# Sliding-window attention and gated MLP: w_in in two halves, three pairs turned by DMA, and another order for the first seventeen slots

## The chip, the cores and the metric

One core of one Trainium2 chip runs one launch. The time is the device time in microseconds; the figure of record is the median of several runs. TensorE (PE) does matmuls and transposes, ScalarE (ACT) the exponentials, the relu and some copies, VectorE (DVE) copies, normalisation and the gate's product, GpSimd (POOL) casts, masks and the weight loads, SyncE (SP) issues most DMAs.

## The reference

```python
scores = scale * np.matmul(q, k.transpose(0, 1, 3, 2))      # 8 batches, 8 heads, 576 x 64
rel = pos[:, None] - pos[None, :]
mask = (rel >= 0) & (rel < 128)
scores = np.where(mask, scores - slope[h] * np.abs(rel), -1e9)
attn = softmax(scores)
x = np.matmul(attn, v)            # to 4608 tokens x 512
h = x @ w_in                      # 512 -> 2048
g = h * np.clip(h + 3.0, 0.0, 6.0) / 6.0
out = g @ w_out                   # 2048 -> 512
```

## The kernel before

The attention goes by 32 slots g: a slot is a batch b = g // 4 and a pair of heads hp = g % 4. In a slot, queries and keys stand transposed in qTb and kTb (64 rows of each head, so a pair fills 128). A window of 128 means that a tile of 128 queries meets two key tiles: the diagonal one (scores into the PSUM tile scd, exponentials into pd) and the one before (sco, po). For batches 0 and 1 the slope and the mask of some tiles are added by matmuls with a table (tables_diag, tables_off); elsewhere POOL masks with affine_select. The products with v land in av, are divided by their sums (avs), turned so that the features lie on partitions, and stored in xT, a ring of four batches.

The MLP goes by nine token tiles nt of 512. Each has 16 up units (moe_up: 4 matmuls of 128x512 from xT and w_in_sb, then ACT's relu L470 and DVE's product L471 into gbuf) and 16 down units (moe_down: 4 matmuls from gbuf and w_out_sb; after each fourth a copy and a store). The list `units` fixes their order from ORDER, and `fill(n)` issues the next n, if the xT that they read is complete (`done`). Everything is issued in an order written out by hand: each engine runs its own instructions strictly in that order, and waits on semaphores.

Loads: the q and k of batch 0 come pair by pair (load_run, k on ACT's queue, q on SP's, eight loads in the order of the pairs 0 to 3), are cast to bf16 (prepare), turned by 36 PE transposes of 64x64 (transposes, L219) and copied to qTb and kTb (L220). Those of batches 1 and 2 come as four-head blocks (load_double, prepare_double, wide_double or double), those from batch 4 on by tokens and a transposing DMA (xbar). Each DMA waits for the eighth before it, whose semaphore it takes over, and SP issues strictly in order. The same space in ldbuf serves batch after batch, so a load also waits for the cast that reads the one before.

w_in comes in four quarters of 512 columns and w_out in four of 512 rows, cast by POOL's DMA queue (L166, L171). In batch 0, pd and po live in w_out_sb, in batch 1 in gbuf[1].

first_batch warms PE with 20 matmuls of 128x128 (L153), adds the tables of slot 0, warms with 10 more, then does transposes(0), scores, exponentials and so on by slot; all four exponentials must be in before attend(3) and back(3), which complete xT for the first up unit. back(g) turns avs by five PE transposes (L432) and one copy for slots 0 to 7, 10 and 11, and by a DMA transpose (L425) for the others; by_xbar tells which. second_batch does slots 4 to 8, segment the rest, one slot after the other, each with seven calls of fill.

Of the kernel before, what the change touches and what calls it, by code (L numbers as in the profile page):

```python
# [18 lines left out]
def kernel(  # L19
# [29 lines left out]
    NB_FULL = 2  # L49
    RING = 4 * S  # L50
# [5 lines left out]
    ident = perm.tile([128, 128], BF16)  # L56
    bias3 = perm.tile([128, 1], FP32)
# [22 lines left out]
    p4buf = [held.tile([128, 2, 128], BF16, name=f"p4buf{i}") for i in range(2)]  # L80
# [94 lines left out]
    def second_w_in():  # L175
        nc.gpsimd.memset(w_out_sb[:, 4, 0:1], 0.0)
        load_w_in(1)

# [24 lines left out]

    def prepare(g, copies):
        for nm, copy in zip("qk", copies):
            pr = prs.tile([128, RT * D], BF16, tag=f"pr{nm}", name="pr",
                          padded_shape=[128, 2 * RT * D])
            copy(out=pr, in_=runs[nm][:, g % NP, :])
            st[g, nm] = pr

    def transposes(g, copies):
        b, hp = divmod(g, NP)
        for nm, dst, copy in (("q", qTb[b % 2], copies[0]), ("k", kTb[b % 2], copies[1])):
            src = st.pop((g, nm))
            tp = ps_h.tile([128, RT, RP], BF16, tag="h", name="tp", padded_shape=[128, 16, 64])
            for t in range(RT):
                for e in range(2):
                    r = slice(e * D, (e + 1) * D)
                    nc.tensor.transpose(tp[r, t, :], src[r, ts(t, D)], ident[r, r])  # L219
            copy(out=dst[:, hp, :, :].rearrange("p j c -> p (j c)")[:, 0:S].rearrange(  # L220
                "p (a t) -> p a t", t=RT), in_=tp.rearrange("p t a -> p a t"))
# [52 lines left out]
    def rooms(g):  # L274
        b, hp = divmod(g, NP)
        if full(g):
# [81 lines left out]
    def exp_off(g, e):  # L358
        h = 2 * (g % NP) + e
        po, sc, p4 = st[g, "po"], st[g, "sco"], p4buf[g % 2]  # L360
# [13 lines left out]
    def av_matmuls(g, qts, where):  # L374
        b, hp = divmod(g, NP)
        vb = vbuf[b % 2]
        pd, po, p4 = st[g, "pd"], st[g, "po"], p4buf[g % 2]
# [135 lines left out]
    ORDER = [("UUDUDUUDUD", "UUDUDUDUD", "UDUDUDD", "UUDDDD"),  # L513
# [3 lines left out]
    for nt in range(1, n_nt + 1):  # L517
        ups, downs = iter(range(16)), iter(range(16))
        for c in "".join(ORDER[0 if nt == 1 else 2 if nt == n_nt else 1]):
            units.append((nt, moe_up, next(ups)) if c == "U" else (nt, moe_down, next(downs)))  # L520
# [36 lines left out]

    def first_batch():
        prepare(0, (V, A))
        warm_up(20)  # L560
        tables_diag(0)
        tables_off(0)
        warm_up(10)
        transposes(0, (V, A))
        scores_diag(0)
        prepare(1, (P, V))
        transposes(1, (V, V))
        scores_off(0)
# [12 lines left out]
        exp_full(2)
        scores_diag(3)
        scores_off(3)
        exp_full(3)
        cast_v(0, 0, V)
        cast_v(0, 1, P)
        load_w_in(0)
        cast_v(0, 2, V)
        cast_v(0, 3, V)
        cast_v(0, 4, P)  # L590
        for dp in range(2):
            for nm in "kq":
                load_double(1, dp, nm, nc.sync)
        load_tokens(1, "v")
        attend(0)
        attend(1)
        back(0)
        attend(2)
        back(1)
        prepare_double(1, 0, (P, P), early=second_w_in)  # L600
        attend(3)
        back(2)
        up_begin(0, 0, 3)
# [160 lines left out]
```

## Time and profile before

| what | value |
|---|---|
| three runs, median | 323.52 us (323.32 to 324.7) |
| profiled execution | 323.3 us |
| its span | 321.6 us |
| mean granted clock of PE | 0.998 |
| DMA issues from launch to landing, q and k of batch 0 | 3.7 to 7.3 us, median 5.4 |
| w_in quarters, issue to landing | 6.3 to 9.5 us, median 8.8 |
| xT by DMA transpose, first six | 2.4 to 4.3 us, median 3.0 |

The span runs from the first to the last instruction of the profiled execution; its time is 1.7 us longer. "Busy" on PE counts a matmul from its start to the modelled end of its result, so two matmuls in a row overlap in it, and a short wait between them can hide under the first one's end. What PE loses is therefore read from the starts. An idle time in square brackets names what ended it.

### The profile page before, as it was taken

How to read it: one execution, taken by the hardware profiler on the slowest of the kernel's cores; microseconds unless marked ns; L12 is line 12 of the kernel's file. 1: busy time of each engine (PE TensorE's matmuls, PEld its weight loads, DVE VectorE, ACT ScalarE, POOL GpSimd, SP SyncE). 2: the span in 40 equal slices, each digit the busy share in tenths (PEclk: the TensorE clock that was granted, in tenths of full speed). 3: DMA queues.
4: the chain of work that ended last, by engine and by line, in shares of the span. 5: the costliest groups of instructions: out<-in, count | busy, mean ns of one | idle time of the engine just before them, and what ended most of it. 6: DMA issues, size and time to landing. Idle time of an engine off the chain costs nothing.

```text
span 321.6 us, 7050 instructions
## 1 busy us (share of the span) xinstructions
PE 312.4 (97%) x2738; PEld 167.6 (52%) x2738; DVE 173.0 (54%) x338; ACT 195.6 (61%) x334; POOL 141.1 (44%) x249
## 2 busy tenths in 40 slices
PE   7889999999999999999999999999999999999996
PEld 5565465455555554554667654554554444444443
DVE  6667674554456555555555555555655455455510
ACT  3758976877767766766676667666764344244401
POOL 8455493594493767366745665463331000000000
PEclk9999999999999999999999999999999999999999
DMA  7999999899999999999999989922112200000112
GB/s 276 202 333 208 247 270 196 210 258 194 212 248 166 244 201 203 193 229 199 192 199 202 237 173 212 214 72 86 23 53 66 75 34 35 33 33 33 67 53 77
DMA packets 131425, 51.90 MB, mean 161 GB/s; under 512 B 118976, under 2 KB 123328, under 8 KB 131392
## 3 DMA queue, kind: packets, MB, share of 16 engines
q1 hardware_dynamic: 126160, 45.36, 66.2%
q0 software_dynamic: 4224, 4.19, 8.2%
q10 hardware_dynamic: 1008, 1.90, 1.6%
q8 instruction: 21, 0.34, 0.5%
q14 instruction: 12, 0.10, 0.1%
HBM read 36.70 MB, written 9.44 MB: 143 GB/s over the span
## 4 chain that ended last, share of the span: by engine, by line
PE 82%; DMA 10%; SPq 2%; POOL 2%; DVE 1%; ACT 1%; issue 1%; POOLq 0%
PE ops L501 37%; PE hps L451 33%; DMA w_out_sb<-in_moe_w_out_dram 5%; DMA ldbuf<-in_v_dram 3%; PE scd L296 3%; DMA ldbuf<-in_k_dram 2%; PE av L391 2%; SPq L112 2%; PE av L383 2%; PE sco L328 1%; PE ops L482 1%; PE w L153 1%; POOL w_out_sb L171 1%; PE tp L219 0%; ACT kTb L244 0%
## 5 line engine op out<-in xcount | busy, mean ns | idle before, releaser
L471 DVE SCALAR_TENSOR_TENSOR gbuf<-r,hps 128x512 bf16<-128x512 f32 x144 | 98.7, 687 | 102.5 <-ACT r L470 100.2
L470 ACT ACTIVATE r<-hps,bias 128x512 f32<-128x512 f32 x144 | 98.9, 689 | 88.9 <-PE hps L451 88.7
L451 PE MATMUL hps<-xT,w_in_sb 128*128 128x512 bf16 (+1 forms) x640 | 144.8, 358 | 0.5 <-ACT xT L438 0.3
L501 PE MATMUL ops<-w_out_sb,gbuf 128*128 128x512 bf16 x560 | 137.8, 379 | 0.3 <-DMA w_out_sb<-in_moe_w_out_dram 0.3
L451 PEld LDWEIGHTS <-w_in_sb 128*128 128x128 bf16 x640 | 59.2, 98 | 54.8 <-issue 0.8
L501 PEld LDWEIGHTS <-gbuf 128*128 128x128 bf16 x560 | 51.8, 98 | 56.7 <-issue 0.6
L354 POOL TENSOR_SCALAR_AFFINE_SELECT pd<-pd 128x512 bf16<-128x512 bf16 x48 | 29.7, 634 | 34.5 <-ACT pd L351 34.5
L364 POOL TENSOR_SCALAR_AFFINE_SELECT po<-po 128x512 bf16<-128x512 bf16 x48 | 30.3, 636 | 32.5 <-ACT po L361 32.3
L351 ACT ACTIVATE pd<-scd,bias_d 128x512 bf16<-128x512 f32 x48 | 31.7, 685 | 4.7 <-PE scd L296 4.7
L510 DVE COPY osb<-ops 128x512 f32<-128x512 f32 x33 | 22.7, 687 | 20.4 <-PE ops L501 20.2
L361 ACT ACTIVATE po<-sco,bias_o 128x512 bf16<-128x512 f32 x48 | 33.0, 688 | 0.0
L194 POOL CAST tbuf<-ldbuf 128x512 bf16<-128x512 f32 (+1 forms) x45 | 25.6, 614 | 16.7 <-DMA qTb<-tbuf 9.0
L402 DVE TENSOR_TENSOR avs<-av,rc 128x384 bf16<-128x384 f32 (+1 forms) x48 | 23.6, 491 | 1.6
L391 PEld LDWEIGHTS <-pd 128*128 128x128 bf16 x192 | 14.3, 97 | 8.3 <-issue 0.5
L383 PE MATMUL av<-vbuf,po 128*128 128x65 bf16 x192 | 18.0, 193 | 0.0
L391 PE MATMUL av<-vbuf,pd 128*128 128x65 bf16 x192 | 17.3, 194 | 0.3 <-ACT kTb L244 0.3
L187 POOL CAST vbuf<-ldbuf 128x1024 bf16<-128x1024 f32 x14 | 14.3, 1044 | 4.3 <-DMA ldbuf<-in_v_dram 4.3
L383 PEld LDWEIGHTS <-po 128*128 128x128 bf16 x192 | 14.3, 98 | 2.9 <-DVE avs L402 0.5
L367 ACT ACTIVATE p4buf<-sco,bias_d 128x64 bf16<-128x64 f32 x48 | 15.5, 324 | 0.0
L227 POOL CAST pr<-ldbuf 128x576 bf16<-128x576 f32 x20 | 12.9, 670 | 5.0 <-DMA ldbuf<-in_k_dram 3.1
L296 PE MATMUL scd<-qTb,kTb 64*128 64x128 bf16 x256 | 12.7, 219 | 1.7 <-DVE kTb L220 0.9
L296 PEld LDWEIGHTS <-kTb 64*128 64x128 bf16 x256 | 7.2, 94 | 13.4 <-issue 9.7
(96 smaller groups left out, 217.4 us busy)
## 6 DMA issues: line engine op xcount, KB each, us to landing
out_dram<-osb SPq DMA_DIRECT2D x33, 256.0 KB, 2.4
ldbuf<-in_v_dram SPq DMA_DIRECT2D x32, 256.0 KB, 5.6
ldbuf<-in_q_dram SPq DMA_DIRECT2D x20, 256.0 KB, 4.9
ldbuf<-in_k_dram SPq DMA_DIRECT2D x16, 256.0 KB, 4.5
ldbuf<-in_q_dram SPq DMA_DIRECT2D x12, 288.0 KB, 7.3
ldbuf<-in_k_dram SPq DMA_DIRECT2D x12, 288.0 KB, 7.6
w_in_sb<-in_moe_w_in_dram POOLq DMA_DIRECT2D x4, 512.0 KB, 8.8
w_out_sb<-in_moe_w_out_dram POOLq DMA_DIRECT2D x4, 512.0 KB, 11.6
```

Of the source, the lines that this page charges most:

```text
L194: nc.gpsimd.tensor_copy(out=tbuf[:m, :, j, :], in_=s[:m, j, :, :].rearrange("p (i e) d -> p i (e d)", e=2))
L296: nc.tensor.matmul(scd[:, e, ts(j, 128)], lhsT=kT[r, j, :], rhs=qT[r, j, :], start=first, stop=first or j == 3)
L351: nc.scalar.activation(out=pd[:, e, :, :].rearrange("p j c -> p (j c)"), in_=sc[:, e, :], func=ACT.Exp, bias=bias_d[:, h:h + 1], scale=scale)
L354: nc.gpsimd.affine_select(out=pd[:, e, :, :], in_=pd[:, e, :, :], pattern=[[0, 4], [1, 128]], channel_multiplier=-1, base=0, compare_op=AL ...
L361: nc.scalar.activation(out=po[:, e, :, :].rearrange("p j c -> p (j c)"), in_=sc[:, e, :], func=ACT.Exp, bias=bias_o[:, h:h + 1], scale=scale)
L364: nc.gpsimd.affine_select(out=po[:, e, :, :], in_=po[:, e, :, :], pattern=[[0, 4], [-1, 128]], channel_multiplier=1, base=-1, compare_op=A ...
L383: nc.tensor.matmul(out_av, lhsT=po[:, e, qt % 4, :], rhs=vb[:, qt - 1, h, :], start=True, stop=False)
L391: nc.tensor.matmul(out_av, lhsT=d, rhs=vb[:, qt, h, :], start=(qt == 0), stop=True)
L451: nc.tensor.matmul(hps[:, lo:hi], lhsT=w_in_sb[:, ks, ts(ms, 128)], rhs=xT[:, ks, ds(src, hi - lo)], start=(ks == 0), stop=(ks == n_ks - 1))
L470: nc.scalar.activation(out=r6, in_=hps, func=ACT.Relu, bias=bias3[:, 0:1], scale=1.0 / 6.0)
L471: nc.vector.scalar_tensor_tensor(out=gts[nt][:, ms, :], in0=r6, scalar=1.0, in1=hps, op0=ALU.min, op1=ALU.mult)
L501: nc.tensor.matmul(ops[nt, sub], lhsT=gts[nt][:, ms, ts(sub, 128)], rhs=w_out_sb[:, ms, :], start=(ms == 0), stop=(ms == n_ms - 1))
```

## The change

first_batch, second_batch and the part of segment up to slot 19 are replaced by a list of steps, PLAN, one step a line. run_plan calls a small function for each. A step's own line names its operands (slot, token tile and unit, PSUM bank, engine: V is DVE, P is POOL, A is ACT). Copies and the PE work that they follow are separate steps now. From slot 20 on the loop of segment goes on as before.

- w_in is loaded by `wp 0 0 4` and `wp 1 0 4`, 128 rows by four k-blocks by 1024 columns each.
- `bx 5`, `bx 6` and `bx 4` give slots 4 to 6 back by a DMA transpose on SP; slot 7 (`bk 7`) stays on PE. 15 transposes of 128x128 and three copies L438 go.
- PE's order begins with 20 warm-up matmuls, the diagonal tables of slot 0 and the transposes of k of pair 2 (`t0 2 k`); then tables of slot 1, q of pair 1, seven warm-ups, k and q of pair 0.
- POOL begins with one memset and the cast `c0 2 k P`. The other memsets come later.
- The eight loads of q and k of batch 0 stay in their order. The v of batch 0 is no longer loaded right behind them, but between the loads of batch 1.
- Batch 0 is normalised into a room in gbuf[0] (avs0), by slot for query tiles 0 to 2 and by rows for the others; the last 64 tokens of it are turned for all slots at once (`br`, `er`).
- Up and down units have another order in token tiles 0 to 2; p4buf has four buffers.
- The steps in short: c0, t0, e0 are cast, PE transposes and copy of one operand of a batch-0 pair; pd, dt, de the same for a four-head block; td, to the tables, sd, so the scores, xt, xd, xo the exponentials, md a mask; vf, vr, vl, at the products with v, nf, nr, nl, na their normalisation; bf, ef and bk, ek turning and copying to xT; u, ur, um the matmuls, relu and product of an up unit (ub its first matmuls only), d a down unit; wu warm-up, mem and cv, vt, ct memsets and casts; ldd, ldt loads on SP; wp, wout the weight loads on POOL.
- Steps that aren't called (`sel`, `lw`, `vu` and others) are left out below.

```diff
+    NB_ROOM = 2
...
-    p4buf = [held.tile([128, 2, 128], BF16, name=f"p4buf{i}") for i in range(2)]
+    p4buf = [held.tile([128, 2, 128], BF16, name=f"p4buf{i}") for i in range(4)]
...
-    def second_w_in():
-        nc.gpsimd.memset(w_out_sb[:, 4, 0:1], 0.0)
-        load_w_in(1)
...
+    avs0 = gbuf[0].rearrange("p m c -> p (m c)")[:, ds(11 * NT, NP * NQ * 128)].rearrange(
+        "p (g j e d) -> p g j e d", g=NP, j=NQ, e=2)
...
-        if full(g):
+        if g < NB_ROOM * NP:
...
-    ORDER = [("UUDUDUUDUD", "UUDUDUDUD", "UDUDUDD", "UUDDDD"),
+    ORDER = [("UUDUDUUDUDUUDUDUDUDUDUDUDDUUDDDD",),
...
-        for c in "".join(ORDER[0 if nt == 1 else 2 if nt == n_nt else 1]):
+        for c in "".join((ORDER[0 if nt == 1 else 2 if nt == n_nt else 1]) if nt != 2 else "DDDDUUDUDUDUDUUDUDUDUDUUDUDUDDUU"):
...
-    def first_batch():
-        prepare(0, (V, A))
-        warm_up(20)
-        tables_diag(0)
-        tables_off(0)
-        warm_up(10)
-        transposes(0, (V, A))
...
-        attend(3)
-        back(2)
-        up_begin(0, 0, 3)
-        back(3)
-        wide_double(1, 0, "q", V)
...
+    def s_c0(g, nm, eng):
+        pr = prs.tile([128, RT * D], BF16, tag=f"pr{nm}", name="pr",
+                      padded_shape=[128, 2 * RT * D])
+        C[eng](out=pr, in_=runs[nm][:, g % NP, :])
+        st[g, nm] = pr
...
+    def s_t0(g, nm, tag):
+        src = st.pop((g, nm))
+        tp = psum(tag, RT * RP, BF16).rearrange("p (t a) -> p t a", t=RT)
+        for t in range(RT):
+            for e in range(2):
+                r = slice(e * D, (e + 1) * D)
+                nc.tensor.transpose(tp[r, t, :], src[r, ts(t, D)], ident[r, r])
+        st["t", g, nm] = tp
...
+    def s_e0(g, nm, eng):
+        dst = (qTb if nm == "q" else kTb)[0]
+        C[eng](out=dst[:, g, :, :].rearrange("p j c -> p (j c)")[:, 0:S].rearrange(
+            "p (a t) -> p a t", t=RT), in_=st.pop(("t", g, nm)).rearrange("p t a -> p a t"))
...
+    def s_ldd(b, dp, nm, e):
+        nc.sync.dma_start(out=ldbuf["qk".index(nm)][:, ds((2 * dp + e) * RT * D, RT * D)],
+                          in_=src_of[nm][b, ds(4 * dp, 4), :, :].rearrange(
+                              "(i e) (a t) d -> e a i (t d)", e=2, t=RT)[e])
...
+    def normed(av, to, n):
+        rc = small.tile([128, 4, 2, 1], FP32, tag="rcn", name="rcn")
+        nc.vector.reciprocal(rc[:, 0:n], av[:, :, :, D:W])
+        nc.vector.tensor_tensor(out=to, in0=av[:, :, :, 0:D],
+                                in1=rc[:, 0:n].to_broadcast([128, n, 2, D]), op=ALU.mult)
...
+    def s_vf(g, tag):
+        av = st["vf", g] = quads(tag, 3)
+        av_matmuls(g, range(3), lambda qt, e: av[:, qt, e, :])
...
+    def s_vl(g):
+        av = st["vl"] = quads("sc", 4)
+        av_matmuls(g, range(4), lambda qt, e: av[:, qt, e, :])
...
+    def s_bf(g, tag):
+        tp = st["bf", g] = psum(tag, 512, BF16)
+        for j in range(4):
+            nc.tensor.transpose(tp[:, ts(j, 128)],
+                                avs0[:, g, j, :, :].rearrange("p e d -> p (e d)"), ident)
...
+    def s_ef(g, lo, n, eng):
+        C[eng](out=xT[:, g, ds(lo, n)], in_=st["bf", g][:, ds(lo, n)])
...
+    def s_u(nt, ms, tag):
+        hps, n = st.get(("u", nt, ms), (None, 0))
+        if hps is None:
+            hps = psum(tag, 512)
+        up_mms(nt, ms, n, n_ks, hps)
+        st["u", nt, ms] = hps, n_ks
+        at[0] += 1
...
+    def s_ur(nt, ms):
+        r6 = st["r", nt, ms] = rpool.tile([128, NT], FP32, tag="r6", name="r6")
+        nc.scalar.activation(out=r6, in_=st["u", nt, ms][0], func=ACT.Relu, bias=bias3[:, 0:1],
+                             scale=1.0 / 6.0)
...
+    def s_um(nt, ms):
+        gts[nt] = gbuf[nt % 2]
+        nc.vector.scalar_tensor_tensor(out=gts[nt][:, ms, :], in0=st["r", nt, ms], scalar=1.0,
+                                       in1=st["u", nt, ms][0], op0=ALU.min, op1=ALU.mult)
...
+    def s_wp(i, k0, n):
+        nc.gpsimd.dma_start(out=w_in_sb[:, ds(k0, n), ts(i, 1024)],
+                            in_=moe_w_in[ds(k0 * 128, n * 128), ts(i, 1024)].rearrange(
+                                "(k p) f -> p k f", p=128))
...
+    def s_bx(g):
+        b, hp = divmod(g, NP)
+        nc.sync.dma_start_transpose(
+            out=xT[:, hp, ds(b % 4 * S, SP)].rearrange("p (j c) -> p j c", j=NQ),
+            in_=st[g, "avs"].rearrange("p j e d -> p (j e d)"))
...
+    def run_plan(text):
+        for line in text.split("\n"):
+            if line.strip():
+                name, *args = line.split()
+                STEPS[name](*(int(a) if a.isdigit() else a for a in args))
...
+    PLAN = """
+mem 1
+c0 2 k P
+c0 1 q V
+wu 20
+td 0
+c0 0 k A
+ldd 1 0 q 1
+t0 2 k av
+ldt 0 v 1
+td 1
+ldd 1 0 k 0
+e0 2 k V
+c0 1 k P
+t0 1 q o
+mem 2
+e0 1 q A
+wu 7
+t0 0 k h
+ldt 0 v 3
+e0 0 k A
+c0 0 q V
+t0 0 q h
+t0 1 k h
+e0 0 q A
+ldd 1 0 q 0
+e0 1 k V
+c0 3 q P
+c0 3 k P
+t0 3 q o
+sd 0
+xt 0
+t0 3 k h
+sd 1
+xt 1
+c0 2 q P
+t0 2 q h
+pd 1 0 q 0 V
+wp 0 0 4
+to 0
+e0 2 q V
+so 0
+mem 3
+pd 1 0 q 1 P
+ldt 0 v 0
+td 2
+e0 3 k V
+ldt 0 v 2
+sd 2
+xo 0
+ldd 1 1 k 0
+to 1
+cv 0 0 V
+xt 2
+cv 0 2 P
+so 1
+xo 1
+to 2
+so 2
+mem 5
+dt 1 0 q 0 9 sc
+cv 0 1 V
+ldd 1 0 k 1
+xo 2
+vf 0 av
+nf 0
+vf 2 h
+ldd 1 1 q 0
+pd 1 0 k 0 V
+e0 3 q A
+ldd 1 1 k 1
+ldd 1 1 q 1
+td 3
+sd 3
+vf 1 av
+nf 1
+cv 0 3 A
+vr 0 3 3 h
+ldt 0 v 4
+nf 2
+de 1 0 q 0 9 A
+xt 3
+nr 0 3 3
+to 3
+so 3
+bf 1 o
+ef 1 0 512 V
+pd 1 0 k 1 P
+dt 1 0 k 0 9 sc
+xo 3
+mem 0
+vl 3
+nl 3
+ldd 2 0 k 1
+bf 2 h
+bf 0 o
+ef 0 0 512 V
+bf 3 av
+de 1 0 k 0 9 A
+wp 1 0 4
+sd 5
+sd 4
+mem 4
+ef 3 0 256 A
+ef 3 256 256 A
+pd 1 1 k 0 P
+ef 2 0 512 V
+xd 5 0
+u 0 0 h
+u 0 1 o
...
+u 0 9 h
...
+at 5
+u 0 10 o
+ldt 2 v 0
+na 5
+bx 5
+xd 7 0
+xd 7 1
+um 0 8
+ur 0 10
+at 6
+na 6
+ldd 3 0 k 0
+ldd 2 1 k 0
+u 0 5 h
+mem 7
+md 7 0
+md 7 1
+pd 2 0 k 1 P
+bx 6
+pd 2 0 q 0 V
+dt 2 0 k 0 5 av
+de 2 0 k 0 5 A
+to 7
+so 7
+xo 7
+um 0 10
+md 4 1
+at 4
+ur 0 5
+vt 2 0
+na 4
+u 0 15 o
+ur 0 15
+dt 2 0 k 5 9 av
+um 0 5
+u 0 14 h
+ldd 2 1 q 0
+pd 2 0 q 1 P
+dt 2 0 q 0 9 sc
+at 7
+de 2 0 k 5 9 V
+de 2 0 q 0 9 A
+u 0 12 h
+um 0 15
+na 7
+ur 0 14
+um 0 14
+wout 0
+pd 3 0 k 0 P
+bx 4
+sd 8
+xd 8 1
+ub 1 0 3 av
+bk 7 sc
+xd 8 0
+ek 7 V
+sd 9
+pd 2 1 k 0 P
+ur 0 12
+u 1 5 h
+pd 2 1 q 0 P
+pd 2 1 q 1 V
+dt 2 1 q 5 9 sc
+ct 3 q 0
+xd 9 1
+ldd 2 1 k 1
+xd 9 0
+md 8 1
+u 1 3 o
+ur 1 5
+um 0 12
+u 1 0 av
...
+u 1 4 av
+de 2 1 q 5 9 A
+pd 2 1 k 1 P
+dt 2 1 k 0 5 h
+d 0 0 0 h
+wout 3
...
+um 3 12
+"""
...
-        load_tokens(0, "v")
...
-        memsets_later()
-        first_batch()
-        second_batch()
-        fill(2)
-        segment(2 * NP, G, lambda g: FILLS.get(g, (1, 1, 1, 2, 0, 1, 2)))
+        run_plan(PLAN)
+        done[0] = 20 - 1
+        segment(20, G, lambda g: FILLS.get(g, (1, 1, 1, 2, 0, 1, 2)))
         done[0] = G
```

1002 lines of the change are left out of this document (881 added, 121 removed).

## The prediction, made before the run

> **What bounds the kernel now.** I read the page first: busy times, then the slices, then the start by timeline.
>
> ```profile
> PE 312.4 (97%) x2738; PEld 167.6 (52%) x2738; DVE 173.0 (54%) x338; ACT 195.6 (61%) x334; POOL 141.1 (44%) x249
> ...
> PE   7889999999999999999999999999999999999996
> ```
>
> PE is busy for 312.4 of 321.6 us, and only the first three slices and the last are below nine tenths. So the change can win little beyond what PE loses early. The windows say how much is visibly idle:
>
> ```profile
> 0.00:20.00 20.00, 16.08 (x322) 11.57 (x323) 12.75 (x45) 11.01 (x13) 11.94 (x29) 1.00 0.98 250
> 20.00:45.00 25.00, 24.21 (x280) 14.01 (x277) 16.72 (x26) 21.00 (x33) 16.05 (x24) 1.00 1.12 273
> 45.00:60.00 15.00, 14.19 (x138) 8.08 (x135) 8.97 (x16) 11.62 (x21) 7.26 (x13) 1.00 1.09 181
> ```
>
> Columns after the length: PE, weight loads, DVE, ACT, POOL, granted clock, DMA share, GB/s. PE idles 3.9 us in the first 20 us, 0.8 and 0.8 in the next stretches. ACT is busy 21.0 of 25 us from 20 to 45: there a second engine is near its limit. From 120 to 300 us PE has no idle time at all, so a delay made before that is carried to the end.
>
> The start, PE's timeline first, then POOL's and ACT's:
>
> ```profile
> 1.43 2.31 PE L153 MATMUL w<-ident 128*128 128x128 bf16 x20 [1.43 <-POOL ident masks.py:199]
> 3.54 1.06 PE L271 MATMUL scd<-tab,ident 128*128 128x512 bf16 x2
> ...
> 5.24 1.27 PE L153 MATMUL w<-ident 128*128 128x128 bf16 x10
> 6.45 0.76 PE L219 MATMUL tp<-ident,pr 64*64 64x64 bf16 x36
> 7.94 0.40 PE L296 MATMUL scd<-qTb,kTb 64*128 64x128 bf16 x8 [0.74 <-ACT kTb L220]
> ```
>
> ```profile
> 7.66 1.63 POOL L208 CAST pr<-ldbuf 128x576 bf16<-128x576 f32 x2 [0.46 <-DMA ldbuf<-in_q_dram]
> ```
>
> ```profile
> 4.72 0.67 ACT L208 CAST pr<-ldbuf 128x576 bf16<-128x576 f32 x1 [0.18 <-DMA ldbuf<-in_k_dram]
> 7.24 0.64 ACT L220 COPY kTb<-tp 128x576 bf16<-128x576 bf16 x1 [1.85 <-PE tp L219]
> 8.38 1.02 ACT L348 ACTIVATE w_out_sb<-scd 128x1024 bf16<-128x1024 f32 x1 [0.49 <-PE scd L296]
> ```
>
> The reader is to see that pair 0 of k is there at 4.72 (its cast waits for the load), that PE begins transposes at 6.45, and that the first exponential runs at 8.38. POOL's row is the cast of q of pair 2, then of k of pair 2: it ends at 7.66 + 1.63 = 9.29, so k of pair 2 is castable at about 8.6. By the landings in the trace, k of the pairs 0 to 3 arrives at 4.70, 6.23, 8.47 and 9.46. The first run of dense up units starts at 23.88 us, 15.5 us behind the first exponential.
>
> **The change, part 1: the start.** PE works in order, and behind the 20 warm-ups and two table matmuls now stands `t0 2 k`, whose input is POOL's `c0 2 k`. The load order is unchanged, so that cast runs from 8.5 to 9.2 (0.67) and the first transposes come at 9.2, not 6.45; PE stands still from about 4.5. What follows, at the rows' durations: 18 transposes 0.4, copy `e0 2 k` on DVE 0.76 (to 10.4); meanwhile PE does tables and `t0 1 q`; `wu 7` needs the bank that e0 2 k frees, 0.4, `t0 0 k` 0.4 (to 11.4); ACT copies k and q of pair 0 one behind the other, 2 x 0.64 (to 12.8, `c0 0 q` on DVE waits behind e0 2 k and is done at 11.0, in time); `sd 0` 0.4. First exponential at 13.3, 4.9 late.
>
> That is at the full rate. The rows of the start show PE at half rate: a 128x128 matmul each 107 ns from 1.43 to 6.2, and 56 ns for the same shape later. It took 4.8 us of work without a break until the faster rate showed. The change works 3.0 us without a break and then waits 4.7. At half rate the five PE pieces between 9.2 and `sd 0` (0.4, 0.43 tables, 0.4, 0.4, 0.4 and the warm-ups) double, which moves the first exponential to about 15.2. Bounds 13.3 and 15.2; I take 14.5, nearer the slow end, since nothing shows the fast rate after so short a run.
>
> The Trainium skill, "TensorE: Matmul & The Clock Gate", Part 1, says that the array is at half rate until about 3.4 us of sustained work and falls back after an idle window as long. By it the end near 15.2 holds and the sum below grows by 0.7; the trace agrees with its two rates (107 and 56 ns), and no run so far shows the falling back.
>
> **Part 2: from the first exponential to the first up unit.** ACT's order is fixed: six exponentials of 1.02, `e0 3 q` 0.64, `cv 0 3` 0.67, `de 1 0 q` 1.11, two exponentials more: 10.6 us with little waiting, since tables and scores of a slot (0.9) fit under another's exponential. Then `vl 3` 0.7, normalising 0.2 + 0.8, `bf` 0.45, two ACT copies of 0.37: 2.9. First dense up unit at 14.5 + 13.5 = 28.0. Before it was 15.5 us behind the first exponential, so 2 us of waits are won back here. 28.0 - 23.9 = 4.1 late. But PE then has less left: 15 transposes L432 of 56 ns (0.84) never come; the rest (two four-head transposes and two sets of scores done early, the last query row and three begun up matmuls still owed) about cancels to 0.3 against. So the true lag is 4.1 - 0.5 = 3.6 us (2.4 at the full rate, 4.3 at half).
>
> **Part 3: w_in in halves.** Twice the bytes, the same 512 pieces. A quarter took 6.3 to 9.5 us to land; two issued together, at 27.83 and 28.56, were both in at 37.98, 10.2 us from the first. A half is bounded by one quarter's best, 6.3, and two times the worst, 19.0; I take 10.2, the row with the same bytes. `wp 0` stands behind `c0 2 q` on POOL, so at 14, landing at 24 (20 to 33), needed at 28. `wp 1` stands behind `pd 1 0 k 1` and is issued at about 24.5, landing at 34.7 (31 to 43.5), needed by `u 0 9`, seven units, two four-head transposes and a set of scores behind the first: 28 + 8 = 36. Cost nothing, cover 1.3 us; the late ends would cost 5 to 7.
>
> **Part 4: slots 4 to 6 by DMA.** Three ACT copies of 0.64 go, in the stretch where ACT is at 21.0 of 25 us. Added are three issues of 1.2 on SP. SP waits with `bx 5` for na 5, with `bx 6` for na 6, with `bx 4` for na 4; behind them stand the loads of batches 2 and 3, whose consumers come 5 us later or more. What is late next is `ub 1 0 3`, whose first matmul reads slot 4. From at 4 to there PE has `u 0 15`, `u 0 14`, `u 0 12` (0.86 each), at 7 0.53, 14 transposes 0.8, `sd 8` 0.3: 4.2 us. Normalising takes 1.0 and the landing 2.4 to 4.3 (as much as 7.3, as loads in a full queue take): 3.4 to 8.3. I take 4.0, the median row of 3.0, as SP stood waiting before it and its queue has emptied: nothing.
>
> **Part 5: the middle.** Adding up the starts in PE's timeline from 24 to 92 us, in ten places a matmul starts 0.18 to 0.49 us later than the one before it needs, 3.1 us in all; three of them, 0.98, are the backs and four-head transposes between 43.9 and 48.3, and one of 0.49 waits for w_out at 58.5, here:
>
> ```profile
> 59.05 1.02 PE L501 MATMUL ops<-w_out_sb,gbuf 128*128 128x512 bf16 x4 [0.33 <-DMA w_out_sb<-in_moe_w_out_dram]
> ```
>
> The first down unit now stands behind 23 up units, not 18, so that wait has cover; the new backs take the 0.98. Against it, `ur 0 0` is behind four exponentials of 0.69 on ACT. Bounds: 3.1 won, or the three loads and casts of part 4 that come late lose the 2.8 of those exponentials. I take 1.3 won.
>
> **Sum.** 323.3 (profiled execution) + 3.6 - 1.3 + 0 + 0 = 325.6. The median is 0.2 above the profiled execution: 325.8.
>
> **The rivals.** Nothing: the full rate holds (lag 2.4) and the middle gives 2.3 back: 323.5. For it: from 120 us on PE is closed, and the ten places are there to be closed. Against it: it needs the good end twice.
>
> Faster, by one mechanism: the third load on ACT's queue lands with the first. Place: `c0 2 k`. If k of pair 2 came at 4.7, the casts would be done at 5.4, the chain 3.8 us sooner and at the rate that unbroken work gives: first exponential 9.5, first up unit 23.0, lag -1.4; with 1.3 from the middle 323.5 - 2.7 = 320.8. It decides if the landing is before about 6.5. For it: all eight loads are launched within 1.4 us of each other. Against it: 4.70, 6.23, 8.47, 9.46, in order.
>
> Slower by more: a transfer comes behind its cover, `wp 1` for `u 0 9` or `bx 4` for `ub 1 0 3`. Price 1 to 7; by the middle of either 3.5: 329.3. For it: the DMA share is 1.0 to 1.1 there, and half a matrix waits for its last piece. Against it: both have 0.2 to 1.3 us of cover by the median rows.
>
> **How the numbers follow.** Forecast 0.46 (its own range 323.8 to 327.6), nothing 0.25, slower by more 0.16, faster 0.13. A measurement of this kernel can tell about 0.5%, 1.6 us, from no change: 321.9 to 325.1. Of the forecast 0.38 lies above that, 0.07 within; nothing gives 0.23 within, 0.01 on either side. Slower 0.38 + 0.16 + 0.01 = 0.55, within 0.30, faster 0.15. The range for 8 in 10 takes in the bounds of the start and part of either outer case: 321.0 to 329.6.
>
> **What would show it.** PE's first transposes at 9.2 with an idle time before them that ends with POOL's cast; matmuls at 107 ns still behind them; the first exponential at 13.3 to 15.2; the first dense up unit near 28; no idle time of PE that ends with w_in or xT's transposing DMA; fewer gaps between 43 and 60 us. I am wrong if the first transposes come before 7 us, if the first up unit comes before 25, or if over 3 us come back in the middle.

## The result, and the profile after

The changed kernel takes 335.78 us (median of four runs, 333.72 to 337.7), the kernel before beside it on the same chip 323.82 us: a ratio of 1.0365, with a 95% interval of 1.0299 to 1.0431. It is 12 us slower, above the range that was forecast. The profiled execution took 335.69 us, its span is 334.0.

The page of the changed kernel first: the span, the busy times, and in 40 slices PE's busy share and granted clock.

```profile
span 334.0 us, 6941 instructions
...
PE 311.3 (93%) x2680; PEld 169.0 (51%) x2720; DVE 171.3 (51%) x345; ACT 197.4 (59%) x337; POOL 135.3 (41%) x242
...
PE   3988994799999999899999999999999999999996
...
PEclk9997999699999999999999999999999999999999
```

PE is busy about as long as before (311.3 us against 312.4; some forty matmul records are missing in this trace), but the span is 12.4 us longer, so PE lost time standing still. The loss has two places: the first slice, and the slices from 50 to 67 us. In two slices the clock is below 9 tenths, each time just behind a wait. PE's timeline names the waits (start, length, and in brackets the idle time and what ended it):

```profile
8.69 0.69 PE L620 MATMUL bank<-ident,pr 64*64 64x64 bf16 x18 [4.09 <-POOL pr L611]
...
25.93 0.68 PE L756 MATMUL wide<-ident,pr 128*128 128x128 bf16 x9 [1.05 <-POOL pr L747]
...
60.14 1.44 PE L433 MATMUL bank<-xT,w_in_sb 128*128 128x512 bf16 x3 [6.13 <-DMA xT<-avs]
...
62.58 0.61 PE L433 MATMUL bank<-xT,w_in_sb 128*128 128x512 bf16 x1
...
137.57 1.24 PE L433 MATMUL bank<-xT,w_in_sb 128*128 128x512 bf16 x4 [1.10 <-DMA xT<-avs]
```

The first row is the start: `t0 2 k` waits for POOL's cast of the third load of k. The third is the large one: the first matmul of token tile 1 (`ub 1 0 3`) waits 6.13 us for slot 4, which `bx 4` brings by the transposing DMA. The first exponential, from ACT's timeline, and the cast of batch 1 behind the wait at 25.93, from POOL's:

```profile
14.40 1.94 ACT L330 ACTIVATE w_out_sb<-scd 128x1024 bf16<-128x1024 f32 x2 [0.73 <-PE scd L278]
```

```profile
25.21 0.66 POOL L747 CAST pr<-ldbuf 128x576 bf16<-128x576 f32 x1 [6.52 <-DMA ldbuf<-in_k_dram]
```

POOL stood still for 6.5 us until that load of k was in. It had been issued at 15.49, and the chain of waits has its whole way, as it has that of `bx 4`:

```profile
15.49 9.60 DMA ldbuf<-in_k_dram
...
51.44 8.66 DMA xT<-avs
```

The windows of the changed kernel (length, then busy time of PE, weight loads, DVE, ACT and POOL, granted clock, DMA share, GB/s):

```profile
20.00:30.00 10.00, 7.80 (x128) 5.46 (x127) 5.47 (x14) 7.17 (x11) 4.68 (x9) 0.85 0.94 253
53.50:65.00 11.50, 5.15 (x34) 2.73 (x35) 3.13 (x5) 4.11 (x7) 6.20 (x10) 0.70 1.21 208
```

In the kernel before, PE was busy for 9.35 us of the first of these windows and 11.04 us of the second, at a clock of 1.00 in both.

To see where the 12 us arise I use a lag: the time at which PE starts an instruction, less the time at which the kernel before started the one with equally much PE work left. (Up to 50 us it reads about 0.8 too low for kernels that give slots 4 to 6 back by DMA: the fifteen transposes are no work of theirs.)

| kernel (profiled execution) | 30 us | 50 us | 66 us | 105 us | 150 us |
|---|---|---|---|---|---|
| changed | 5.5 | 5.3 | 12.9 | 10.7 | 12.6 |
| changed, slots 4 to 6 back on PE (e1) | 4.0 | 5.2 | 4.3 | 2.8 | 3.3 |
| the order alone (e9) | 4.1 | 5.1 | 4.5 | 4.1 | 4.7 |
| start's queues mended (e15) | 2.0 | 4.9 | 4.0 | 2.5 | 3.2 |

So the changed kernel loses 5.3 at the start, 7.6 from 50 to 66 us, wins 2.2 back until 105, loses 1.9 more until 141 (1.10 of it in the last row of the timeline above), and nothing from there on: 323.3 + 12.6 = 335.9, against 335.7 profiled.

### The profile page after: what moved, and what is told of

The parts are those of the page before. It is cut to its first block, busy times and chain, and to the rows that moved or that the text cites. A ratio compares the mean times of both kernels' runs of the same rounds, so it can differ in the third digit from the quotient of the medians.

```text
span 334.0 us, 6941 instructions
## 1 busy us (share of the span) xinstructions
PE 311.3 (93%) x2680; PEld 169.0 (51%) x2720; DVE 171.3 (51%) x345; ACT 197.4 (59%) x337; POOL 135.3 (41%) x242
## 4 chain that ended last, share of the span: by engine, by line
PE 83%; DMA 9%; issue 1%; POOL 1%; DVE 1%; ACT 1%; SPq 0%; POOLq 0%
PE ops L483 24%; PE hps L433 21%; PE bank L433 14%; PE bank L791 9%; DMA xT<-avs 4%; DMA ldbuf<-in_k_dram 3%; PE scd L278 2%; PE av L373 2%; PE av L365 2%; PE sco L310 2%; DMA kTb<-tbuf 1%; PE ops L464 1%; DMA out_dram<-osb 1%; PE wide L756 1%; PE bank L620 1%
## 5 line engine op out<-in xcount | busy, mean ns | idle before, releaser
L452 ACT ACTIVATE r<-hps,bias 128x512 f32<-128x512 f32 x83 | 57.2, 689 | 65.6 <-PE hps L433 64.6
L483 PE MATMUL ops<-w_out_sb,gbuf 128*128 128x512 bf16 x354 | 87.5, 379 | 1.5 <-issue 1.0
L453 DVE SCALAR_TENSOR_TENSOR gbuf<-r,hps 128x512 bf16<-128x512 f32 x83 | 57.1, 688 | 59.9 <-ACT r L452 59.0
L433 PE MATMUL hps<-xT,w_in_sb 128*128 128x512 bf16 (+1 forms) x390 | 82.5, 344 | 0.2
L433 PE MATMUL bank<-xT,w_in_sb 128*128 128x512 bf16 x228 | 60.2, 387 | 8.3 <-DMA xT<-avs 7.2
L784 DVE SCALAR_TENSOR_TENSOR gbuf<-r,bank 128x512 bf16<-128x512 f32 x61 | 41.0, 684 | 31.6 <-ACT r L779 31.3
L779 ACT ACTIVATE r<-bank,bias 128x512 f32<-128x512 f32 x61 | 41.2, 690 | 19.9 <-PE bank L433 18.4
L791 PE MATMUL bank<-w_out_sb,gbuf 128*128 128x512 bf16 x177 | 43.3, 379 | 0.1
L346 POOL TENSOR_SCALAR_AFFINE_SELECT po<-po 128x512 bf16<-128x512 bf16 x24 | 15.2, 636 | 20.2 <-ACT po L343 20.2
L904 POOL TENSOR_SCALAR_AFFINE_SELECT po<-po 128x512 bf16<-128x512 bf16 x24 | 15.2, 636 | 19.7 <-ACT po L898 17.4
L937 POOL CAST tbuf<-ldbuf 128x512 bf16<-128x512 f32 (+1 forms) x25 | 14.6, 613 | 12.5 <-issue 7.4
L898 ACT ACTIVATE po<-sco,bias_o 128x512 bf16<-128x512 f32 x24 | 16.4, 688 | 3.0 <-PE sco L310 3.0
```

The source lines that it names most:

```text
L433: nc.tensor.matmul(hps[:, lo:hi], lhsT=w_in_sb[:, ks, ts(ms, 128)], rhs=xT[:, ks, ds(src, hi - lo)], start=(ks == 0), stop=(ks == n_ks - 1))
L452: nc.scalar.activation(out=r6, in_=hps, func=ACT.Relu, bias=bias3[:, 0:1], scale=1.0 / 6.0)
L453: nc.vector.scalar_tensor_tensor(out=gts[nt][:, ms, :], in0=r6, scalar=1.0, in1=hps, op0=ALU.min, op1=ALU.mult)
L483: nc.tensor.matmul(ops[nt, sub], lhsT=gts[nt][:, ms, ts(sub, 128)], rhs=w_out_sb[:, ms, :], start=(ms == 0), stop=(ms == n_ms - 1))
L779: nc.scalar.activation(out=r6, in_=st["u", nt, ms][0], func=ACT.Relu, bias=bias3[:, 0:1], scale=1.0 / 6.0)
L784: nc.vector.scalar_tensor_tensor(out=gts[nt][:, ms, :], in0=st["r", nt, ms], scalar=1.0, in1=st["u", nt, ms][0], op0=ALU.min, op1=ALU.mult)
```

## The experiments

Each kernel ran beside the kernel before. Ratios are to that kernel, with their 95% interval. Edits are to the changed kernel where nothing else is said.

### The three slots that go back by DMA

**e1_backs_pe**: slots 4 to 6 back on PE, the rest as changed.

```diff
-bx 5
...
+bk 5 av
+ek 5 A
...
-bx 6
+bk 6 av
+ek 6 A
...
-bx 4
+bk 4 av
+ek 4 A
```

> Slots 4 to 6 go back by five PE transposes and an ACT copy each, as before the change; all else as changed (335.8 us). Theory A, the first matmul of token tile 1 waits for slot 4's transposing DMA (6.1 us idle, then half rate): the wait and some 2 us at half rate go, 15 transposes of 56 ns (0.84) come back: 328.5. Rival B, the queue of SP is late as a whole, and q of batch 2's second block (landed 59.4) is waited for instead, a few steps on: only about 3 us are won, 332.5.

Measured: 327.98 us, 1.0135 (1.0097 to 1.0174). The transposing DMA costs 7.8 of the 12 us by the medians, 7.4 by the ratios. PE is busy for 10.92 of the 11.5 us from 53.5 to 65, at a clock of 1.00.

**e2_wout_late**: the first quarter of w_out is issued after `bx 4`, not ahead of it.

```diff
-wout 0
 pd 3 0 k 0 P
 bx 4
...
 pd 2 1 q 0 P
+wout 0
 pd 2 1 q 1 V
```

> The first w_out load is issued later on POOL, behind a cast that needs the landing of batch 2's q block, so that nothing of w_out moves while slots 5, 6 and 4 are transposed by DMA. Theory C, the weight load takes the DMA engines from SP's queue: slot 4 lands within 4.3 us of its issue instead of 8.7, PE waits 1 us or less, 329.5, unless the down units then wait for w_out. Rival, the transposing DMA itself is slow or serial: slot 4 lands as late as now, 335.8 or more.

Measured: 331.94 us, 1.0266 (1.0228 to 1.0303). PE's timeline of this kernel, the lines with waits:

```profile
55.04 0.81 PE L433 MATMUL bank<-xT,w_in_sb 128*128 128x512 bf16 x3 [1.64 <-DMA xT<-avs]
63.69 1.04 PE L791 MATMUL bank<-w_out_sb,gbuf 128*128 128x512 bf16 x4 [0.79 <-DMA w_out_sb<-in_moe_w_out_dram]
68.29 1.89 PE L791 MATMUL bank<-w_out_sb,gbuf 128*128 128x512 bf16 x8 [2.04 <-DMA w_out_sb<-in_moe_w_out_dram]
75.85 2.75 PE L791 MATMUL bank<-w_out_sb,gbuf 128*128 128x512 bf16 x12 [1.13 <-DMA w_out_sb<-in_moe_w_out_dram]
```

The wait for slot 4 falls from 6.13 to 1.64 us, but the down units now wait three times for w_out, 4.0 us in all. The view of the DMA issues says the same in one row each (what, queue, kind, how many, size, median us from issue to landing), for 45 to 62 us. The changed kernel:

```profile
q1 hardware_dynamic: 6111, 2.58, 79.4%
q0 software_dynamic: 528, 0.52, 28.5%
...
xT<-avs SPq DMA_TRANSPOSE x3, 7.1
```

and this one:

```profile
xT<-avs SPq DMA_TRANSPOSE x3, 4.2
```

The same three transposes land in 4.2 us, by the median, without a w_out quarter under way and in 7.1 us with it. `bx 5` took 2.7 us in both kernels, ahead of that load; `bx 6` and `bx 4` took 4.9 and 4.2 us here, 7.15 and 8.66 in the changed kernel. The two queue rows of the changed kernel give packets, MB and the packets' share of 16 engines' time. The weight load's 528 packets of about 1 KB take 28.5% of 17 us on 16 engines, so 147 ns each; SP's 6111 of about 0.4 KB take 79.4%, so 35 ns each. Together that is 107.9%, more than the engines have: packets overlap in time, and these are durations, not times in which an engine served one packet alone.

**e5_keep_warm**: 100 warm-up matmuls where PE waits for slot 4.

```diff
+wu 100
 ub 1 0 3 av
```

> The changed kernel, with 100 warm-up matmuls of 128x128 on PE ahead of the first matmul of token tile 1, where PE waits 6.1 us for slot 4. Theory F, the 2 us lost behind that wait are PE at half rate after it stood still: the wait stays, the matmuls behind it come each 216 ns at once, 333.8. Rival, the 2 us are other waits of the same queue: 335.8.

Measured: 331.01 us, 1.0248 (1.0203 to 1.0292), 4.8 us less than the changed kernel by the medians and 3.8 by the ratios, by work that serves nothing. PE's timeline of this kernel at the place:

```profile
51.52 5.76 PE L156 MATMUL w<-ident 128*128 128x128 bf16 x100
57.34 0.81 PE L433 MATMUL bank<-xT,w_in_sb 128*128 128x512 bf16 x3
```

The three matmuls behind the wait take 0.81 us here and 1.44 in the changed kernel. From 57 to 65 us this kernel's lag doesn't grow, where the changed kernel's grows by 2.0 between 60.1 and 66.6: so 2.0 of the 4.8 us is PE's lower clock behind the wait. Another 2.1 was there ahead of the edit (lag at 50 us without the added matmuls 3.2, not 5.3): this kernel had no wait at 25.93 and a clock of 1.00 from 20 to 30. The load of k behind that wait was issued at 14.70 and landed at 23.39 us here, 15.49 and 25.09 in the changed kernel. Why, with the same instructions up to there, stays open; the changed kernel's four runs themselves spread over 4 us.

**e6_before_xbar**: the kernel before, with slots 4 to 6 back by DMA and the loads of batches 2 and 3 moved behind the three transposes.

```diff
-        return g >= XB and g != XB + 2 and g != XB + 3
+        return NP <= g < XB - 1 or g >= XB and g != XB + 2 and g != XB + 3
...
-        load_tokens(2, "v")
         prepare_double(2, 1, (P, P))
-        for dp in range(2):
-            load_double(3, dp, "k", nc.sync)
-        load_tokens(3, "q")
...
         back(NP + 2)
+        load_tokens(2, "v")
+        for dp in range(2):
+            load_double(3, dp, "k", nc.sync)
+        load_tokens(3, "q")
```

> The kernel before, with slots 4 to 6 given back by the transposing DMA alone, and the loads of v of batch 2, k and q of batch 3 on SP moved behind them so that they don't stand ahead in the queue. Theory C, the w_out load takes the DMA engines from SP's queue: before, a v load issued at 47.95 landed at 59.2 while w_out moved, so the transposes issued at 45 to 48 land late, PE waits 5 to 10 us at the first matmuls of token tile 1, 329 to 334. Rival, the long landing belongs to the changed order of loads: PE waits 1 us or less and saves 0.84, 323.

Measured: 340.59 us, 1.0534 (1.0492 to 1.0575), more than expected. Its DMA issues from 40 to 62 us and the place in PE's timeline:

```profile
w_out_sb<-in_moe_w_out_dram POOLq DMA_DIRECT2D x4, 512.0 KB, 11.7
...
xT<-avs SPq DMA_TRANSPOSE x3, 10.8
```

```profile
57.04 1.12 PE L254 MATMUL tp<-ident,pr 128*128 128x128 bf16 x9 [8.28 <-DVE avs L413]
```

Here all four quarters of w_out are on their way when the first two transposes are issued, and no load of SP moves beside them; they take 10.8 and 12.2 us. The third, issued at 57.01 as the last quarter comes in, takes 2.6. The wait is one step further back: avs has two buffers, each is held until its transposing DMA has read it, so DVE cannot normalise the next slot, and PE stops behind DVE. The loads moved behind the transposes then come late as well; from 75 us on the lag is over 17 us.

### w_in in halves

**e4_quarters**: w_in in four quarters, two issued at each of the two places.

```diff
-wp 0 0 4
+win 0
+win 1
...
-wp 1 0 4
+win 2
+win 3
```

> w_in in four quarters again, issued in the places of the two halves. Theory E, a half is one long transfer that holds back SP's loads (k of batch 1, landed 25.1, for which PE waits 1.2 us): quarters let it through earlier, 334.5. Rival, the bytes count and not the pieces: within 0.7 of 335.8.

Measured: 333.74 us, 1.0312 (1.0283 to 1.0341): 2.0 us less than the changed kernel, with intervals that overlap. The wait at 25.93 is gone; that for slot 4 is 6.94. But e1 and e5 load w_in in halves and have no wait there either, so the runs don't show that the quarters took it away.

**e9_order_alone**: quarters and PE for slots 4 to 6 together, so that only the order is left of the change (the edits of e1 and e4).

> What is left of the change is the other order of the work: slots 4 to 6 go back on PE and w_in comes in quarters, two at each of the two places. Theory A with B (the three parts add up): with the backs on PE the changed kernel took 328.0, and quarters were worth 2.0, so 326.0. Rival (the two gains are the same one, since both free the DMA engines near the first up unit): 328.0, no less than with the backs on PE alone.

Measured: 328.27 us, 1.015 (1.0114 to 1.0186). With the backs on PE, quarters gain nothing against halves (328.27 and 327.98). The rival holds: the two gains don't add. Of the 12 us the halves are therefore worth 0 to 2, and what the order costs by itself is 5.

**e7_before_halves**: the kernel before with w_in in two halves.

```diff
-            out=w_in_sb[:, :, ts(g, 512)],
-            in_=moe_w_in[:, ts(g, 512)].rearrange("(k p) f -> p k f", p=128))
+            out=w_in_sb[:, :, ts(g, 1024)],
+            in_=moe_w_in[:, ts(g, 1024)].rearrange("(k p) f -> p k f", p=128))
...
-        load_w_in(2)
-        load_w_in(3)
```

> The kernel before, with w_in in two halves, issued where the first and the second quarter were. Theory G, a half lands some 10 us after its issue: at 22.5 to 24, by when the first up matmuls stand at 22.0; PE loses 0 to 2 us, 323.8 to 325.5. Rival, half a matrix takes its bytes' time behind SP's loads, twice a quarter's 8.2: landing near 29, PE loses 5, 328.5.

Measured: 326.71 us, 1.0105 (1.007 to 1.014), 3.8 us over the kernel before in the same session (322.95). PE's timeline of this kernel:

```profile
24.04 0.82 PE L451 MATMUL hps<-xT,w_in_sb 128*128 128x512 bf16 x3 [2.57 <-DMA w_in_sb<-in_moe_w_in_dram]
```

In this order the half is needed at once and lands 11.7 us after its issue. Behind the wait the clock is 0.60 and 0.54 from 25 to 29 us, so the loss is longer than the wait; in the changed order the first up units come so late that PE never waits for w_in itself.

### The start

**e3_load_order**: the eight loads of batch 0 in the order in which the plan casts them.

```diff
-        load_run(0, "k", nc.scalar)
-        load_run(0, "q", nc.sync)
-        load_run(1, "k", nc.scalar)
-        load_run(1, "q", nc.sync)
-        for g in (2, 3):
-            load_run(g, "k", nc.scalar)
-            load_run(g, "q", nc.sync)
+        for gk, gq in ((2, 1), (0, 0), (1, 3), (3, 2)):
+            load_run(gk, "k", nc.scalar)
+            load_run(gq, "q", nc.sync)
```

> The eight loads of batch 0 come in the order in which the plan casts them: k 2, 0, 1, 3 on ACT's queue and q 1, 0, 3, 2 on SP's. Theory D, the first transposes wait for the third load: they come at about 5.3 instead of 8.7, and the start gives back 3 us and more. If the later wait for slot 4 moves along with PE's work, the time is 332.5; if that wait is paced by the DMA queues (rival), PE only waits longer there and the time stays within 0.7 of 335.8.

Measured: 335.32 us, 1.0345 (1.0308 to 1.0383): no gain. The lines with waits of PE's timeline:

```profile
5.63 0.69 PE L620 MATMUL bank<-ident,pr 64*64 64x64 bf16 x18 [1.03 <-POOL pr L611]
...
16.66 0.40 PE L278 MATMUL scd<-qTb,kTb 64*128 64x128 bf16 x8 [2.66 <-DVE qTb L625]
...
22.92 0.19 PE L373 MATMUL bank<-vbuf,w_out_sb 128*128 128x65 bf16 x1 [1.83 <-POOL vbuf L180]
```

The first transposes come 3.1 us sooner, as meant. But DVE has the cast of batch 1's q ahead of the copy that `sd 2` needs, and that load landed at 15.07; and v of batch 0 landed at 22.19, behind the half of w_in. The lag is 0.1 at 11 us and 6.2 at 30.

**e8_start_and_backs**: PE for slots 4 to 6, quarters, the loads in the plan's order, four loads of v at the head of SP's list, and the casts of batch 1's q behind the copy for `sd 2`.

```diff
+ldt 0 v 0
+ldt 0 v 1
+ldt 0 v 2
+ldt 0 v 3
 mem 1
...
-pd 1 0 q 0 V
...
-pd 1 0 q 1 P
...
 e0 3 k V
+pd 1 0 q 0 V
+pd 1 0 q 1 P
```

> The changed kernel with slots 4 to 6 back on PE, w_in in quarters, the loads of batch 0 in the plan's order, the first four v loads of batch 0 ahead of batch 1's on SP, and the two casts of batch 1's first q block behind the copies of pairs 2 and 3. If the start is held by the loads alone (theory D): first transposes at 5.6, the lag of 4 us at 30 us shrinks to 1 or less, 324 to 325. If by the order of work on ACT and PE (rival): no gain over the run with slots 4 to 6 on PE, 328.

Measured: 332.34 us, 1.0268 (1.0235 to 1.0301). The lag is 0.5 at 15 us; then PE waits once, for batch 1's q, whose loads landed at 19.6 and 22.3 behind two quarters of w_in issued at 10.9 and 11.8:

```profile
23.25 1.12 PE L756 MATMUL wide<-ident,pr 128*128 128x128 bf16 x9 [7.63 <-DVE pr L747]
```

**e10_spread**: the order alone (e9), with each quarter issued only where its columns come next. The sixteen up units of token tile 0 are renumbered in the order in which they run, so that a quarter serves four in a row.

```diff
-win 0
-win 1
+win 0
...
 pd 1 0 k 1 P
+win 1
...
-win 2
-win 3
+win 2
...
 pd 1 1 q 1 P
+win 3
```

> As the kernel with the order alone, but each quarter of w_in is issued only where its columns come next: the second behind `pd 1 0 k 1`, the fourth behind `pd 1 1 q 1`, and the sixteen up units of token tile 0 are renumbered in the order in which they run. Theory F (weight loads that are issued early hold back what is needed first): 324.5 to 325.5, and no wait of PE for POOL's or DVE's casts of batch 1 between 20 and 30 us. Rival (the early lag is the third load of k alone): the same time as the order alone, within 0.5.

**e11_spread_loads**: that, with the loads in the plan's order (the edit of e3).

> As the spread kernel, with the eight loads of batch 0 in the order in which the plan casts them (k of pair 2 and q of pair 1 first). Theory F: the first transposes at 5.6, and since only one quarter of w_in moves before 20 us, the loads of v and of batch 1 are in time; 322.5 to 324. Rival (the start has a limit in bytes: batch 0, batch 1's first half and two quarters have to be in before the first up units, whatever the order): no better than the spread kernel, with waits for v or batch 1 between 15 and 25 us that take the gain back.

**e12_warm_start**: e9 with 40 more warm-up matmuls in the idle time at the start.

```diff
+wu 40
 t0 2 k av
```

> As the kernel with the order alone, with 40 more warm-up matmuls of 128x128 ahead of the first transposes, in the idle time from 4.4 to 8.7; they are at half rate for some 2 us, so they end at about 7.5, ahead of the cast. Theory H (1.2 us of the start's lag is the half rate that follows the wait): PE runs at 56 ns a matmul from about 7 us on, the first exponential comes at 13.3 to 13.6 instead of 14.4, and the time falls by 0.8 to 1.2. Rival (the copies on ACT and DVE set the chain there, and the half rate is hidden): first exponential and time move by less than 0.4.

Measured: e10 328.35 us, 1.0147 (1.0101 to 1.0193); e11 328.27 us, 1.0153 (1.0116 to 1.019); e12 334.51 us, 1.0365 (1.0311 to 1.0418), its profiled execution 329.59. None is better than the order alone. In e11 the first exponential comes at 11.25 rather than 14.5, and then PE waits 3.02 us at 16.84 for DVE, which has the cast of batch 1's q in front again. In e12 PE's timeline shows the rate, and what takes the gain back (this is the fastest of its five runs, which lie between 329.59 and 336.46 us):

```profile
8.90 0.47 PE L620 MATMUL bank<-ident,pr 64*64 64x64 bf16 x18 [2.05 <-POOL pr L611]
...
22.64 0.19 PE L373 MATMUL bank<-vbuf,w_out_sb 128*128 128x65 bf16 x1 [2.14 <-POOL vbuf L180]
```

Eighteen transposes take 0.47 us behind the added matmuls, though PE waits 2.05 us between, and 0.69 in the changed kernel. The first exponential comes at 13.06 instead of 14.5. So the slow rate is real and worth 1.5 us at this point; but v of batch 0 is not there any sooner.

**e13_queue_order** and **e14_queue_warm**: the queues of the start mended together, on top of e11; e14 also has 12 more warm-up matmuls.

```diff
 t0 2 k av
 ldt 0 v 1
+ldt 0 v 0
+ldt 0 v 2
+ldd 1 0 q 1
+ldd 1 0 q 0
+ldt 0 v 3
+ldd 1 0 k 0
...
-pd 1 0 q 0 V
-win 0
...
 cv 0 2 P
+win 0
...
-dt 1 0 q 0 9 sc
 cv 0 1 V
+pd 1 0 q 0 V
+pd 1 0 q 1 P
...
 vf 2 h
+dt 1 0 q 0 9 sc
```

> As the spread kernel with the loads in the plan's order, and on top: SP loads the v of batch 0 ahead of batch 1's k and q, the casts of q of batch 1 stand behind those of q, k and v of batch 0 on DVE and POOL, the first quarter of w_in is issued only when v is in (about 15 us), and the four-head transposes of q of batch 1 stand behind the values of slots 0 and 2. Theory K (the 4.9 us are the order of the queues at the start): no wait over 1 us of PE after the first transposes, lag at 30 us under 2.5 instead of 4 to 6, and 325 to 326.5. Rival (it is the plan's own chain, over ACT, whatever the loads do): lag of 4 at 30 us and 328 again.

> As that kernel, with 12 more warm-up matmuls ahead of the first transposes, in the wait of 1.2 us there. Theory H (a part of the start's lag is PE's half rate): the transposes take 0.47 instead of 0.69 from the first on, and 0.3 to 0.8 us less than the kernel without them. Rival (what follows waits for copies and loads): the same within 0.3.

Measured: 330.65 us, 1.0235 (1.0211 to 1.0259), and 331.91 us, 1.0262 (1.0245 to 1.0279). Neither tells anything of the question. I had moved `ldd 1 0 q 0` ahead of `c0 0 q V`, which reads the space that the load writes: slot 0 got the queries of batch 1, and the cast waited for that load until 14.5 us, PE with it for 5.81.

**e15_queue_order** and **e16_queue_warm**: the same with that one load behind the cast.

```diff
-ldd 1 0 q 0
 ldt 0 v 3
...
 c0 0 q V
+ldd 1 0 q 0
```

> As e13_queue_order, with the load of q of batch 1 into pair 0's space issued behind the cast of pair 0's q (in e13_queue_order it stood ahead, and slot 0 used the queries of batch 1). Theory K (the 4.9 us are the order of the queues at the start): first exponential at 11 to 11.5, no wait of PE over 1 us between 7 and 25 us, lag at 30 us under 2.5 instead of 4 to 6, and 325 to 326.5. Rival (the plan's own chain over ACT, or the bytes that have to be in by then, whatever the order): lag of 4 or more at 30 us and 328 again.

> As e15_queue_order, with 12 more warm-up matmuls ahead of the first transposes. Theory H (half rate): first transposes at 0.47 instead of 0.69 for eighteen, and 0.3 to 0.8 us less than e15_queue_order. Rival: the same within 0.3.

Measured: 327.06 us, 1.0101 (1.006 to 1.0143), and 326.67 us, 1.0086 (1.0052 to 1.012). The first exponential comes at 11.26, no wait between 7 and 25 us is over 0.9, and the lag at 30 us is 2.0, as expected. The time is not: the lag is back at 4.9 by 50 us, most of it between 41 and 46, where PE waits for v of batch 1, here in PE's timeline of e15:

```profile
42.62 0.19 PE L373 MATMUL wide<-vbuf,gbuf 128*128 128x65 bf16 x1 [1.05 <-POOL vbuf L645]
```

The twelve warm-up matmuls are worth 0.4 us between the medians, which the intervals don't separate.

**e17_late_quarters** and **e18_late_quarters_v**: e15 with the third and fourth quarter of w_in later; e18 also with 12 warm-up matmuls and a load of batch 2 behind the v of batch 1.

```diff
-win 2
...
-win 3
+win 2
...
 md 6 1
+win 3
```

> As e15_queue_order, with the third quarter of w_in issued where the fourth was (26 us) and the fourth behind `md 6 1` (37 us). Theory F (weight loads hold back SP's loads): the v of batch 1 lands before 34 us rather than at 34.5 to 41.5, PE's wait at 42 goes, the lag at 50 us is 3 instead of 4.9, and 1.5 to 2 us less than e15_queue_order: 325.2. Rival (v has to come through the eight places of SP's queue anyhow): the wait stays within 0.5, the same time. A second risk: the fourth quarter is late for unit 12, which would show as a wait of PE for w_in at 45 to 48.

> As e17_late_quarters, with the load of k of batch 2 that held SP from 24.3 to 30.6 behind the v of batch 1, and 12 more warm-up matmuls ahead of the first transposes. Theory F: v of batch 1 in by 32 us; the start 0.3 sooner; 324.5 to 325. This would be the changed plan with its start mended and the backs on PE; it beats the kernel before only if the middle's gain, 2 us in the kernels with the backs on PE, is more than the lag at 50 us, and I expect it not to.

Measured: 326.94 us, 1.0126 (1.0073 to 1.0179), and 327.06 us, 1.0103 (1.0073 to 1.0134). The wait for v is gone. In its place, from PE's timeline of e17:

```profile
45.25 1.04 PE L433 MATMUL bank<-xT,w_in_sb 128*128 128x512 bf16 x4 [2.21 <-DMA w_in_sb<-in_moe_w_in_dram]
```

The fourth quarter, issued at 36.87, landed at 45.21. The lag is 1.9 at 40 us and 4.9 at 50, as it was. No version beats the kernel before; the nearest, e16, is 0.5 to 1.2% slower.

## Why the prediction was wrong

The direction was right, the size not: 335.8 against 325.8. The step that failed is **part 4**, "the median row of 3.0, as SP stood waiting before it and its queue has emptied: nothing".

- **Part 4.** Forecast 4.0 us from `at 4` to landing, of which 3.0 for the transfer, and no cost. `bx 4` was issued at 51.44 and landed at 60.10, 8.7 us later, outside the bounds of 2.4 to 7.3. PE waited 6.13 us, and ran at a lower clock behind it (0.50 from 60 to 64 us, 0.84 from 64 to 66), 2.0 more; by the lag 7.6 of the final 12.6. The premise was wrong twice. SP's queue was not empty: loads of k and q issued at 48.78 and 50.76 landed at 54.13 and 59.41, and the second kept SP from issuing `bx 4` when `na 4` was done, at 50.73. And the DMA engines were shared with `wout 0`, issued at 50.11 on POOL's queue and landed at 59.60, which e2 shows to be what took most of the time: without it the transfer took 4.2 us and PE waited 1.64. I had taken the landing from a quiet stretch of the trace. The right row stood in the same trace of the kernel before, in the DMA issues from 45 to 60 us, while its own w_out load was under way:

```profile
ldbuf<-in_v_dram SPq DMA_DIRECT2D x4, 256.0 KB, 11.4
```

- **The rival that came true** is "a transfer comes behind its cover", with the place that it named, `bx 4` for `ub 1 0 3`. Its price of 1 to 7 left out the clock: 6.13 + 2.0 = 8.1. It had 0.16.
- **Part 1** was right, and with the mechanism: first transposes 8.69 (forecast 9.2), first exponential 14.40 (14.5), the eighteen transposes at 0.69 instead of 0.47 us. That the exponential came so close has some luck in it: the transposes came 0.5 sooner, and the chain behind them took 5.7 us, not 5.3. The long wait is not what makes PE slow there. The two table matmuls ahead of it already take 1.06 us, where two take 0.60 in e12, and in e3 the transposes take 0.69 behind a wait of only 1.03. PE had worked 3.0 us without a break, where the kernel before needed 4.8 to show the faster rate, as part 1 says; with 40 matmuls more (e12) the transposes take 0.47. (The clock row reads 1.00 there and doesn't show this.) Behind the wait for slot 4 PE did fall back from the faster rate, 1.44 us against 0.81. The Trainium skill, "TensorE: Matmul & The Clock Gate", Part 1, has the array fall back to half rate after an idle window of about 3.4 us. The wait of 6.13 us agrees; that of 4.09 tests nothing, as PE was slow ahead of it. Shorter waits do not sort by their length: behind 2.05 in e12 and 2.21 in e17 the rate stayed, behind 2.57 in e7 the clock fell to 0.60, and behind the 1.05 at 25.93 it was 0.52 from 27 to 29 us.
- **Part 2** failed in this execution by a cost of part 3. From the first exponential to the first dense up unit (29.57) it took 15.2 us, not 13.5, and the lag at 30 us was 5.5, not 3.6. But in e1 and e5, which have the same instructions up to there, it took 13.1 and 13.0: the 2 us that "are won back here" came. In them the load of k of batch 1 was in by 23.62 and 23.39 us, not 25.09, and PE had neither the wait at 25.93 nor the lower clock behind it.
- **Part 3** gave the right landings (25.13 and 35.99 against 24 and 34.7), and PE never waited for w_in. What it left out is what else those bytes hold up: the load of k of batch 1, issued 1.7 us behind the first half, took 9.6 us, POOL stood 6.5 us in front of its cast, and `wp 1` behind that cast went out at 26.07. "Cost nothing" became 0 to 2.0 us: 2.0 by e4, nothing by e9 against e1. But e5, with halves, was 2.1 ahead at 50 us, so the 2.0 may be no more than the spread of that load's landing.
- **Part 5** had the right sign and a near size: 2.2 us came back between 66 and 105 us, forecast 1.3; it was 1.5 in e1 and 0.4 in e9, and from which gaps it came isn't shown. Against it stand 1.9 lost from 105 to 141 us, 1.10 in a second wait for a transposing DMA (issued 132.60, landed 137.53), which I had not looked for that far back.
- The order alone, costed at 3.6 - 1.3 = 2.3 and 0.84 for the fifteen transposes that come back, 3.1, costs 5 (e9). Its start is a chain of limits and not one: take away the late load of k (e3), the slow rate (e12) or the cast of q that DVE has in front (e8), and other waits of 2 to 8 us follow; issuing the quarters later (e10) gains nothing by itself. Mending them together (e15) halves the lag at 30 us and moves the loss to 42 to 45 us. What the runs show is that each order so far has some transfer late; that none could do better is argued from the DMA share alone, 0.90 to 1.18 in every window up to 60 us of e9 to e18, and not shown.

## What to carry to other kernels

Take a transfer's landing time from a stretch of the trace in which the same other transfers are under way, the weight loads of another queue among them; a median over quiet places is no price. Ask of every DMA that is issued early whose landing it delays, not only whether its own reader is covered. And a wait of PE can cost more than its length: count the lower clock behind it.

## What the runs showed of the hardware

- SP's transfers and POOL's weight loads share the DMA engines, and a packet of the weight load takes longer: 147 ns for about 1 KB against 35 for about 0.4 KB in the changed kernel from 45 to 62 us. Two transposing DMAs landed in 4.9 and 4.2 us with no quarter of w_out under way (e2), in 7.15 and 8.66 with one (changed), two in 10.8 and 12.2 with four and no load of SP (e6). The Trainium skill, "DMA: Bandwidth & Descriptors", Queues, rings and completion order, has each engine take turns between its queues packet by packet; the unequal packets fit that, though no run here counts the turns.
- 5.76 us of useless matmuls in a wait made the kernel faster, since the clock stayed at 1.00: 2.0 us of the 4.8 are traced to that.
- The granted clock moves with the run: the kernel with a warmed start took 329.59 us at a clock of 1.0 and 334.06 at 0.99, with the same instructions. What decides it between runs, and which of the two brings the other, stays open.
